# Decoding 64-bit weights by half words: raw loads two bytes off a word, one step of the decode on ScalarE

## The chip, the core and the metric

The kernel runs on one core of a Trainium2 chip. The metric is the device time of one execution in microseconds; the time before is the median of three runs.

## What is computed

An attention block masked by clusters feeds two expert layers without routing:

```
x = attention(q, k, v, centroids)                 # 1536 tokens x 512
h = x @ w_in;  g = h * sigmoid(1.702 h);  x = g @ w_out      # 512 -> 2048 -> 512
h = x @ w_in2; r = max(h, 0);             x = (r*r) @ w_out2
```

All inputs are float32 by value, but the four expert weights arrive as 64-bit floats. Before a weight can be multiplied it is turned into a 32-bit float on the chip with integer operations: keep the sign, clamp the magnitude to the range of a 32-bit float, rebias the exponent, shift the fraction.

## The kernel before

**Stages.** Attention takes the first 242 us or so. The expert layers follow as 32 slots: 2 layers x 2 batch halves x 8 pairs of hidden chunks (q = 0 to 31). A slot multiplies tokens with w_in for two hidden chunks (PSUM tiles `ph` and `ps`, L143 or L977), passes them through the activation (`active`, L840: ScalarE reads PSUM and writes `gh` and `h`), takes the rounding rest `gl` on VectorE (`low`, L851), and multiplies with w_out into `y` (L865 to L871). Every product is made of three float32r products of high and low parts. A slot has two halves of one `ph` bank each; a bank can be written again only once `active` has read it.

**Weights.** There are 64 weight chunks of 128 x 512 elements, 512 KB each. `w_dma` (L76) loads one from HBM into one of three buffers `raw64` from SyncE's queue. `magnitude` (L85) makes ScalarE write the absolute value of the high words into the target tile. `decode` (L90) does the four VectorE steps below, one at a time when the slot's hand-written order calls `step(k)` (L1018). The target is `wb` (a w_in chunk that stays), `rr`/`room` (the rest), or for four chunks in attention the raw buffer itself. Then a w_in chunk is stored to HBM by `keep` (L125) and split into `wxh` (ScalarE cast, L946) and `wxl` (VectorE, L947); a w_out chunk is split into `oh` and `ol` (`parts`, L108). `step` calls `fetch` (L996), the next raw load, when a decode is over.

```
nc.scalar.activation(f32(t), f32(raw)[:, :, 1], ACTF.Abs)            # L87  ScalarE
tensor_scalar(tf, tf, E_LO, E_HI, max, min)                          # L96  clamp
tensor_scalar(t, t, 3, 0x3FFFFFF8, shift_left, and)                  # L98  shift
scalar_tensor_tensor(t, high, 0xC0000000, t, and, or)                # L101 sign bits
scalar_tensor_tensor(t, low, 29, t, shift_right, or)                 # L104 fraction
```

**Order.** The order on each engine is written by hand (`manual_schedule`), instructions of an engine run in that order, and waits are semaphores between engines. Four chunks are decoded during attention and a fifth at its end (L797). `COUNTS` (L981) says how many are decoded in each later slot: 2 in slot 0, 4 in each of slots 1 to 6, 1 in slot 7, then 1 to 3 in slots 8 to 23 (3 in slots 9 and 18). Slots 0 to 7 are plain; from slot 8 on a slot uses sums of weights (`sums`, L937, VectorE into `wt`) to save products. In slots of layer 1 ScalarE first copies a product out of PSUM through a Relu (L845).

Of the kernel before, what the change touches and what calls it, by code (L numbers as in the profile page):

```python
# [11 lines left out]
F32 = mybir.dt.float32  # L12
BF16 = mybir.dt.bfloat16
U32 = mybir.dt.uint32
F32R = mybir.dt.float32r
ACTF = mybir.ActivationFunctionType
ALU = mybir.AluOpType
# [8 lines left out]

E_LO = float(np.uint32(0x38000000).view(np.float32))
E_HI = float(np.uint32(0x47EF0000).view(np.float32))


def f32(ap):
    return ap.bitcast(F32)
# [3 lines left out]
def tile_kernel(ctx, tc, q, k, v, cent, w_in1, w_out1, w_in2, w_out2, cw_cols, out):  # L36
    nc = tc.nc
    B, H, S, D = q.shape
    C = cent.shape[1]
    NT, DM = out.shape  # L40
    DFF = w_out1.shape[0]

    w_in1, w_out1, w_in2, w_out2 = (w.bitcast(U32) for w in (w_in1, w_out1, w_in2, w_out2))
    P = 128
    NJ = S // P
    G = 2
    KD = DM // P
# [7 lines left out]
    xpool = ctx.enter_context(tc.tile_pool(name="xpool", bufs=1))  # L55
    rpool = ctx.enter_context(tc.tile_pool(name="rpool", bufs=1))
    t3_p = ctx.enter_context(tc.tile_pool(name="t3", bufs=8))
    wraw_p = ctx.enter_context(tc.tile_pool(name="wraw", bufs=1))
    tmp_p = ctx.enter_context(tc.tile_pool(name="tmpw", bufs=1))
# [8 lines left out]


    x1 = [xpool.tile([P, KD, S], F32, name=f"x1_{b}") for b in range(B)]  # L70


    def raw_tile(at):
        return (wraw_p, wraw_p, tmp_p)[at].tile([P, DM, 2], U32, tag=f"raw{at}", name="raw64")

    def w_dma(w, fc, first, at):  # L76
        raw = raw_tile(at)
        if first:
            nc.sync.dma_start(raw.rearrange("p (a n) t -> p a (n t)", a=KD),
                              w[:, 2 * fc * P:2 * (fc + 1) * P].rearrange("(a p) f -> p a f", p=P))  # L80
        else:
            nc.sync.dma_start(raw.rearrange("p n t -> p (n t)"), w[fc * P:(fc + 1) * P, :])
        return raw

    def magnitude(raw, t):  # L85

        nc.scalar.activation(f32(t), f32(raw)[:, :, 1], ACTF.Abs)  # L87
        return raw, t

    def decode(raw, t, steps=range(4), inside=False):  # L90

        low, high, tf = raw[:, :, 0], raw[:, :, 1], f32(t)
        for i in steps:
            if i == 0:

                nc.vector.tensor_scalar(out=tf, in0=tf, scalar1=E_LO, scalar2=E_HI, op0=ALU.max, op1=ALU.min)  # L96
            elif i == 1:
                nc.vector.tensor_scalar(out=t, in0=t, scalar1=3, scalar2=0x3FFFFFF8,  # L98
                                        op0=ALU.logical_shift_left, op1=ALU.bitwise_and)
            elif i == 2:  # L100
                nc.vector.scalar_tensor_tensor(out=t, in0=high, scalar=0xC0000000, in1=t,  # L101
                                               op0=ALU.bitwise_and, op1=ALU.bitwise_or)
            else:
                nc.vector.scalar_tensor_tensor(out=low if inside else t, in0=low, scalar=29, in1=t,  # L104
                                               op0=ALU.logical_shift_right, op1=ALU.bitwise_or)
        return tf

    def parts(tf, hi, lo, engine=nc.gpsimd, held=None):  # L108

        nc.scalar.copy(hi, tf)  # L110
        rest = lambda: engine.tensor_tensor(out=lo, in0=tf, in1=f32(hi), op=ALU.subtract)
        if held is None:
            rest()
        else:
            held.append(rest)
# [692 lines left out]
    with ExitStack() as actx:  # L808
        w1, raw, xs, mags, first, last_norm = attention(actx)
# [180 lines left out]
    wo = {(0, 0): w1[2:]}  # L990
# [49 lines left out]
    keep(0, 2, f32(mags[4][1]))  # L1040
    weights[1].plain(0, f32(mags[4][1]).rearrange("p (a n) -> p a n", a=2))
    wo[0, 1] = out_tiles(1)
    parts(f32(mags[3][0])[:, :, 0], *wo[0, 1], nc.vector)
    fetch()
    fetch()

# [5 lines left out]
    for q, (layer, b, p) in enumerate(slots):  # L1052
# [3 lines left out]
        n = COUNTS[q] if q < len(COUNTS) else 0  # L1056
# [20 lines left out]
        if q + 2 < 2 * NP and q in PLAIN and q or q >= 2 * NP - 1 and more:  # L1077
            at = q + 1 + (q in PLAIN)
# [271 lines left out]
```

## Time and profile before

| what | value |
|---|---|
| time, median of 3 runs | 754.14 us (753.55 to 754.98) |
| the profiled execution's own time | 753.29 us |
| its span in the profile | 751.5 us |
| TensorE busy | 745.2 us, 99% |
| VectorE busy | 592.1 us, 79% |
| ScalarE busy | 504.0 us, 67% |
| GpSimd busy | 163.0 us, 22% |
| clock granted to TensorE | 1.00 in every stretch |

The span runs from the first to the last instruction; the 1.8 us between span and time lie around it. A busy share is an average over stages of different make-up, so the shares are read again by stretch below. In the trace lists, a row has the start, the duration, the engine, the line, the operation, what it writes and reads, and in brackets how long the engine stood idle before it and for whom it waited. A matmul's listed duration is longer than its step to the next one, because matmuls overlap.

### The profile page before, as it was taken

What the parts mean: (1) busy time and instruction counts of PE and PEld (TensorE: products, weight loads), DVE (VectorE), ACT (ScalarE), POOL (GpSimd) and SP (SyncE); (2) the same over time, 40 slices, a digit from 0 to 9 for tenths busy, and PEclk for the clock granted to TensorE, in tenths of its full rate; (3) what the DMA queues carried; (4) which work ended last, traced back from release to release, by engine and by line L of the source; (5) the groups of instructions that cost most, each with busy time, mean ns of one, the idle gap of its engine ahead of it and who ended that gap; (6) DMA issues with size and microseconds to landing.
All of it is one profiled execution on the core that took longest, in us unless ns stands there. A gap on an engine that the chain in (4) does not pass through costs nothing.

```text
span 751.5 us, 12136 instructions
## 1 busy us (share of the span) xinstructions
PE 745.2 (99%) x4345; PEld 684.6 (91%) x4345; DVE 592.1 (79%) x1079; ACT 504.0 (67%) x1049; POOL 163.0 (22%) x221
## 2 busy tenths in 40 slices
PE   8999999999999999999999999999999999999997
PEld 5999999999999999999999999998998989989996
DVE  7999999989897888887988877888878886643441
ACT  7999999999898644543765554676656675644441
POOL 5748667568654100000000000000000000000000
PEclk9999999999999999999999999999999999999999
DMA  9796796874320845555453432314442204011002
GB/s 206 189 205 145 141 202 179 175 188 109 83 59 12 231 141 173 160 158 172 151 155 124 139 123 91 113 43 136 159 140 85 84 29 140 29 31 54 1 1 84
DMA packets 72092, 90.90 MB, mean 121 GB/s; under 512 B 30368, under 2 KB 54080, under 8 KB 71936
## 3 DMA queue, kind: packets, MB, share of 16 engines
q1 hardware_dynamic: 71488, 89.99, 43.2%
q8 instruction: 34, 0.56, 0.3%
q14 instruction: 26, 0.21, 0.1%
q10 hardware_dynamic: 544, 0.13, 0.1%
HBM read 61.12 MB, written 13.94 MB: 100 GB/s over the span
## 4 chain that ended last, share of the span: by engine, by line
PE 97%; DVE 1%; ACT 1%; POOL 0%; issue 0%; POOLq 0%
PE ps L977 23%; PE y L871 18%; PE y L865 12%; PE pa L546 9%; PE pt L521 8%; PE y L867 6%; PE ps L497 5%; PE ph L143 4%; PE ps L499 4%; PE ps L143 4%; PE ps L350 1%; PE pt L287 1%; PE pm L376 1%; PE y L143 1%; PE ps L360 0%; DVE nm L503 0%
## 5 line engine op out<-in xcount | busy, mean ns | idle before, releaser
L534 DVE TENSOR_TENSOR el<-pt,eh 128x384 fp32r<-128x384 f32 x192 | 97.4, 549 | 7.2 <-ACT eh L531 6.4
L503 DVE TENSOR_REDUCE nm<-ps 128x1 f32<-128x768 f32 x96 | 91.4, 953 | 12.8 <-PE ps L499 10.8
L512 ACT ACTIVATE e<-ps,nm 128x768 f32<-128x768 f32 x96 | 87.8, 915 | 3.2 <-DVE nm L503 2.5
L531 ACT CAST eh<-pt 128x384 fp32r<-128x384 f32 x192 | 83.3, 490 | 7.3 <-PE pt L521 6.0
L848 ACT ACTIVATE gh<-h 128x384 fp32r<-128x384 f32 (+1 forms) x58 | 38.3, 660 | 68.6 <-DVE h L838 38.7
L852 DVE TENSOR_TENSOR gl<-h,gh 128x384 fp32r<-128x384 f32 (+1 forms) x104 | 67.0, 645 | 17.7 <-ACT h L849 9.9
L521 PE MATMUL pt<-identF,e 128*128 128x128 f32 x576 | 80.1, 274 | 0.1
L871 PE MATMUL y<-oh,gl 128*128 128x512 f32 x192 | 75.2, 392 | 0.0
L871 PE MATMUL y<-ol,gh 128*128 128x512 f32 x192 | 75.1, 391 | 0.0
L871 PE MATMUL y<-oh,gh 128*128 128x512 f32 x192 | 74.7, 389 | 0.0
L497 PE MATMUL ps<-k,q 128*128 128x512 f32 x192 | 68.9, 362 | 0.8 <-ACT e L512 0.8
L521 PEld LDWEIGHTS pt<-identF,e 128*128 128x128 f32 x576 | 65.3, 140 | 2.3 <-DVE el L534 1.4
L499 PE MATMUL ps<-k,q 80*128 80x512 f32 x192 | 60.8, 340 | 0.0
L947 DVE TENSOR_TENSOR wxl<-wb,wxh 128x512 fp32r<-128x512 f32 x37 | 25.5, 690 | 40.3 <-ACT wxh L946 31.7
L865 PE MATMUL y<-gh,ol 128*128 128x512 f32 x128 | 50.0, 391 | 0.0
L865 PE MATMUL y<-gh,oh 128*128 128x512 f32 x128 | 50.0, 391 | 0.0
L865 PE MATMUL y<-gl,oh 128*128 128x512 f32 x128 | 50.0, 391 | 0.0
L977 PE MATMUL ps<-xl,wxh 128*128 128x384 f32 x192 | 49.0, 336 | 0.0
L977 PE MATMUL ps<-xh,wxh 128*128 128x384 f32 x192 | 49.0, 336 | 0.0
L977 PE MATMUL ps<-xh,wxl 128*128 128x384 f32 x192 | 48.9, 335 | 0.0
L838 DVE CUSTOM_DVE_ANT_0 h<-ps,h 128x384 f32<-128x384 f32 x48 | 25.7, 552 | 29.0 <-PE ps L977 29.0
L546 PE MATMUL pa<-eh,v 128*128 128x384 f32 x192 | 47.3, 361 | 0.0
(233 smaller groups left out, 1921.2 us busy)
## 6 DMA issues: line engine op xcount, KB each, us to landing
raw<-in_moe_w_in_dram SPq DMA_DIRECT2D x32, 512.0 KB, 4.2
raw<-in_moe_w_out_dram SPq DMA_DIRECT2D x32, 512.0 KB, 3.7
wb<-wst SPq DMA_DIRECT2D x24, 512.0 KB, 3.3
q<-k SPq DMA_DIRECT2D x15, 384.0 KB, 5.6
wst<-room SPq DMA_DIRECT2D x16, 256.0 KB, 2.2
wst<-wb SPq DMA_DIRECT2D x13, 256.0 KB, 2.4
k<-k SPq DMA_DIRECT2D x16, 192.0 KB, 5.9
rawv<-in_v_dram SPq DMA_DIRECT2D x8, 384.0 KB, 7.3
```

Of the source, the lines that this page charges most:

```text
L143: nc.tensor.matmul(ph, w[a][:, kc * P:(kc + 1) * P], xs[kc][z][:, i * QB:(i + 1) * QB], start=(j == 0), stop=(j == len(terms) - 1))
L497: nc.tensor.matmul(ps[:, a:a + n], q2[:, qs], k2[:, a:a + n], start=True, stop=False)
L499: nc.tensor.matmul(ps[:, a:a + n], q1[0:K1, qs], k1[0:K1, a:a + n], start=False, stop=True)
L503: nc.vector.tensor_reduce(out=nm, in_=live["s", t][:, 0:S], op=ALU.max, axis=AX, negate=True)
L512: nc.scalar.activation(e, live["s", t][:, 0:S], ACTF.Exp, bias=live.pop(("nm", t)), accum_out=sums[:, s:s + 1])
L521: nc.tensor.transpose(pt[:, i], e[:, kc * P:(kc + 1) * P], identF)
L531: nc.scalar.copy(place("eh", t, u), live["pt", t, u])
L534: nc.vector.tensor_tensor(out=place("el", t, u), in0=live.pop(("pt", t, u)), in1=f32(place("eh", t, u)), op=ALU.subtract)
L546: nc.tensor.matmul(pa, v2[:, i % NJ, :], src[:, i % NJ, :], start=(i == 0), stop=(i == 2 * NJ - 1))
L865: nc.tensor.matmul(y[m], l[:, cs], r[:, 0:512], start=first, stop=last)
L871: nc.tensor.matmul(y[m], l[:, m * P:(m + 1) * P], r, start=(begin and z == 0), stop=(fc == KF - 1 and z == 2))
L977: nc.tensor.matmul(ps, w[a][:, wi, kc * P:(kc + 1) * P], x[z][kc], start=start and j == kc == 0, stop=j == 2 and kc == 1, skip_group_check ...
```

## The change

The raw buffer gets one more pair of words, and the load puts the 64-bit numbers two bytes behind a word boundary, as 16-bit elements. Each number is then cut differently: its top 16 bits lie at the start of a word of their own with the next number's first bits behind them, and the word before holds the 32 bits under them. ScalarE takes the absolute value of the top half words alone (as bf16) into a contiguous 16-bit tile `code`; VectorE clamps that tile of half words; ScalarE turns the half words into whole numbers with scale 2^19 and a bias from a new tile `base` (Identity, written as int32), which puts exponent and first fraction bits in place; VectorE then sets the rest of the fraction (shift right by 13, or) and, in a last operation on half words, the sign. One VectorE instruction of each of the 64 decodes goes, one ScalarE instruction comes. `base` is set once on GpSimd.

```diff
+STEP, BASE = float(2**19), float(0x3800 * 2**19)
...
-    w_in1, w_out1, w_in2, w_out2 = (w.bitcast(U32) for w in (w_in1, w_out1, w_in2, w_out2))
+    w_in1, w_out1, w_in2, w_out2 = (w.bitcast(U16) for w in (w_in1, w_out1, w_in2, w_out2))
...
+    base = xpool.tile([P, 1], F32, name="base")
+    nc.gpsimd.memset(base, -BASE)
...
-        return (wraw_p, wraw_p, tmp_p)[at].tile([P, DM, 2], U32, tag=f"raw{at}", name="raw64")
+        return (wraw_p, wraw_p, tmp_p)[at].tile([P, DM + 1, 2], U32, tag=f"raw{at}", name="raw64")
...
     def w_dma(w, fc, first, at):
         raw = raw_tile(at)
+        dst = raw.rearrange("p n t -> p (n t)").bitcast(U16)[:, 1:1 + 4 * DM]
...
-            nc.sync.dma_start(raw.rearrange("p n t -> p (n t)"), w[fc * P:(fc + 1) * P, :])
+            nc.sync.dma_start(dst, w[fc * P:(fc + 1) * P, :])
...
+    def words(raw):
+        top = raw.rearrange("p n t -> p (n t)").bitcast(U16).rearrange("p (n t) -> p n t", t=4)[:, 1:, 0]
+        return raw[:, 0:DM, 1], top
     def magnitude(raw, t):
-        nc.scalar.activation(f32(t), f32(raw)[:, :, 1], ACTF.Abs)
+        code = t.bitcast(U16)[:, DM:]
+        nc.scalar.activation(code.bitcast(BF16), words(raw)[1].bitcast(BF16), ACTF.Abs)
     def decode(raw, t, steps=range(4), inside=False):
...
             if i == 0:
-                nc.vector.tensor_scalar(out=tf, in0=tf, scalar1=E_LO, scalar2=E_HI, op0=ALU.max, op1=ALU.min)
+                size = code.bitcast(BF16)
+                nc.vector.tensor_scalar(out=size, in0=size, scalar1=E_LO, scalar2=E_HI, op0=ALU.max, op1=ALU.min)
             elif i == 1:
-                nc.vector.tensor_scalar(out=t, in0=t, scalar1=3, scalar2=0x3FFFFFF8,
-                                        op0=ALU.logical_shift_left, op1=ALU.bitwise_and)
+                nc.scalar.activation(t.bitcast(I32), code, ACTF.Identity, scale=STEP, bias=base)
             elif i == 2:
-                nc.vector.scalar_tensor_tensor(out=t, in0=high, scalar=0xC0000000, in1=t,
+                nc.vector.scalar_tensor_tensor(out=to, in0=rest, scalar=13, in1=t,
+                                               op0=ALU.logical_shift_right, op1=ALU.bitwise_or)
+            else:
+                half = high if inside else t.bitcast(U16)[:, 1::2]
+                nc.vector.scalar_tensor_tensor(out=half, in0=top, scalar=0x8000, in1=half,
                                                op0=ALU.bitwise_and, op1=ALU.bitwise_or)
```

The changed kernel's lines are numbered anew: L98 is the absolute value (before L87), L110 the clamp, L112 the new Identity, L114 the fraction, L118 the sign. Everything behind `decode` stands 14 lines further down: L862 and L863 are `active`, L866 `low`, L960 and L961 the split of w_in, L859 the Relu. TensorE's and SyncE's orders are as before.

Three places show what moves. First, ScalarE in a half of a plain slot, from one `wxh` cast to the next; before:

```order
L946 CAST wxh<-wb 128x512
L87 ACTIVATE wb<-raw_4252 128x512
L848 ACTIVATE gh<-ps 128x384
L849 ACTIVATE h<-ps 128x384
L87 ACTIVATE rr<-raw_4326 128x512
L848 ACTIVATE gh<-ps 128x384
L849 ACTIVATE h<-ps 128x384
L110 CAST oh<-rr 128x512
L946 CAST wxh<-wb 128x512
```

and with the change:

```order
L960 CAST wxh<-wb 128x512
L98 ACTIVATE wb<-raw_4254 128x512
L112 ACTIVATE wb<-wb,base 128x512
L862 ACTIVATE gh<-ps 128x384
L863 ACTIVATE h<-ps 128x384
L98 ACTIVATE rr<-raw_4328 128x512
L112 ACTIVATE rr<-rr,base 128x512
L862 ACTIVATE gh<-ps 128x384
L863 ACTIVATE h<-ps 128x384
L124 CAST oh<-rr 128x512
L960 CAST wxh<-wb 128x512
```

The Identity stands right behind the absolute value, ahead of the activation that frees the next `ph` bank, and between the two lies VectorE's clamp.

Second, VectorE in such a half, from `wxl` to the end of the second decode; before:

```order
L947 TENSOR_TENSOR wxl<-wb,wxh 128x512
L96 TENSOR_SCALAR wb<-wb 128x512
L98 TENSOR_SCALAR wb<-wb 128x512
L852 TENSOR_TENSOR gl<-h,gh 128x384
L101 SCALAR_TENSOR_TENSOR wb<-raw_4087,wb 128x512
L104 SCALAR_TENSOR_TENSOR wb<-raw_4087,wb 128x512
L96 TENSOR_SCALAR rr<-rr 128x512
L98 TENSOR_SCALAR rr<-rr 128x512
L852 TENSOR_TENSOR gl<-h,gh 128x384
L101 SCALAR_TENSOR_TENSOR rr<-raw_4161,rr 128x512
L104 SCALAR_TENSOR_TENSOR rr<-raw_4161,rr 128x512
```

and with the change:

```order
L961 TENSOR_TENSOR wxl<-wb,wxh 128x512
L110 TENSOR_SCALAR wb<-wb 128x512
L866 TENSOR_TENSOR gl<-h,gh 128x384
L114 SCALAR_TENSOR_TENSOR wb<-raw_4089,wb 128x512
L118 SCALAR_TENSOR_TENSOR wb<-raw_4089,wb 128x512
L110 TENSOR_SCALAR rr<-rr 128x512
L866 TENSOR_TENSOR gl<-h,gh 128x384
L114 SCALAR_TENSOR_TENSOR rr<-raw_4163,rr 128x512
L118 SCALAR_TENSOR_TENSOR rr<-raw_4163,rr 128x512
```

One instruction per decode is gone; the `gl` that remains between the clamp and the next step is that of the earlier bank.

Third, ScalarE in slot 18, around the third decode; before:

```order
L848 ACTIVATE gh<-h 128x768
L849 ACTIVATE h<-h 128x768
L87 ACTIVATE room<-raw_6707 128x512
L946 CAST wxh<-wt 128x512
L845 ACTIVATE h<-ps 128x384
```

and with the change:

```order
L862 ACTIVATE gh<-h 128x768
L863 ACTIVATE h<-h 128x768
L98 ACTIVATE room<-raw_6709 128x512
L112 ACTIVATE room<-room,base 128x512
L960 CAST wxh<-wt 128x512
L859 ACTIVATE h<-ps 128x384
```

The Identity now stands ahead of the `wxh` cast and of the Relu copy that frees a PSUM bank, and the clamp that it waits for stands on VectorE behind the four sums of `wt` and a `gl`.

## Rows read from the trace of the kernel before

**Rows 1.** The page's part 1: busy time, share of the span and instructions by engine.

```profile
PE 745.2 (99%) x4345; PEld 684.6 (91%) x4345; DVE 592.1 (79%) x1079; ACT 504.0 (67%) x1049; POOL 163.0 (22%) x221
```

**Rows 2.** The page's part 4: engine shares of the chain that ended last.

```profile
PE 97%; DVE 1%; ACT 1%; POOL 0%; issue 0%; POOLq 0%
```

**Rows 3.** TensorE's waits by line and releaser: us in total, times, longest.

```profile
PE pz L194 <- DVE zeros L188: 1.2, 1, 1.2
PE ps L497 <- ACT e L512: 0.8, 1, 0.8
```

**Rows 4.** Busy time by stretch: us, busy by engine, clock, DMA share, GB/s.

```profile
120.00:200.00 80.00, 80.00 (x558) 75.62 (x558) 71.56 (x122) 74.90 (x178) 54.13 (x71) 1.00 0.64 152
...
300.00:400.00 100.00, 100.00 (x577) 93.75 (x577) 84.52 (x158) 55.10 (x108) 0.00 (x0) 1.00 0.49 157
```

**Rows 5.** ScalarE's groups by line, shapes kept apart: xcount, busy us, mean ns.

```profile
L87 ACT ACTIVATE room<-raw 128x512 f32<-128x512 f32 x32 | 21.6, 675 | 0.0
...
L301 ACT ACTIVATE full<-pt,kq_scale 128x384 f32<-128x384 f32 x27 | 16.1, 598 | 0.0
...
L356 ACT COPY st<-ps 128x384 f32<-128x384 f32 x14 | 6.8, 486 | 0.3
```

**Rows 6.** VectorE's decode lines: ns min/median/max, first and last start.

```profile
L96 DVE TENSOR_SCALAR room<-room x32: 414/418/428, 368.0 to 602.5; 128x512 f32<-128x512 f32 x32
...
L98 DVE TENSOR_SCALAR room<-room x32: 426/428/430, 368.4 to 603.0; 128x512 uint32<-128x512 uint32 x32
...
L101 DVE SCALAR_TENSOR_TENSOR room<-raw,room x32: 681/685/693, 368.9 to 605.2; 128x512 uint32<-128x512 uint32 x32
...
L101 DVE SCALAR_TENSOR_TENSOR wb<-raw,wb x13: 681/686/2217, 249.1 to 346.3; 128x512 uint32<-128x512 uint32 x13
```

**Rows 7.** ScalarE at a plain half slot's start: start us, us, instruction, idle before.

```profile
310.48 0.62 ACT L946 CAST wxh<-wb 128x512 fp32r<-128x512 f32 x1 [2.21 <-PE ph L143]
```

**Rows 8.** All engines in the first slot, 240 to 259 us.

```profile
241.58 0.20 ACT L794 ACTIVATE warm<-identF 128x1 f32<-128x1 f32 x1
...
252.06 0.62 ACT L946 CAST wxh<-wb 128x512 fp32r<-128x512 f32 x1 [2.41 <-DVE wb L104]
...
256.32 0.51 ACT L849 ACTIVATE h<-ps 128x384 f32<-128x384 f32 x1
...
242.36 0.69 DVE L104 SCALAR_TENSOR_TENSOR raw<-raw,raw 128x512 uint32<-128x512 uint32 x1
...
243.08 0.41 SPq L79 DMA_DIRECT2D raw<-in_moe_w_in_dram  x1
...
244.36 0.85 PE L143 MATMUL y<-xh,wyh 128*128 128x384 f32 x4
...
258.92 0.85 PE L143 MATMUL ph<-xh,wxh 128*128 128x384 f32 x4
```

**Rows 9.** All engines in slot 7, 357 to 359 us.

```profile
358.25 0.48 ACT L849 ACTIVATE h<-ps 128x384 f32<-128x384 f32 x1
...
357.27 0.43 DVE L96 TENSOR_SCALAR rr<-rr 128x512 f32<-128x512 f32 x1 [0.73 <-ACT rr L87]
...
358.54 0.68 DVE L101 SCALAR_TENSOR_TENSOR rr<-raw,rr 128x512 uint32<-128x512 uint32 x1
...
358.82 0.93 PE L143 MATMUL ph<-xh,wxh 128*128 128x384 f32 x4
```

**Rows 10.** All engines in slot 18, 535 to 538 us.

```profile
537.02 0.49 ACT L845 ACTIVATE h<-ps 128x384 f32<-128x384 f32 x1 [0.98 <-PE ps L977]
...
535.91 0.95 DVE L852 TENSOR_TENSOR gl<-h,gh 128x768 fp32r<-128x768 f32 x1
...
537.86 0.51 PE L977 MATMUL ps<-xh,wxh 128*128 128x384 f32 x2
```

**Rows 11.** The page's part 6, weight loads: xcount, KB each, us to landing.

```profile
raw<-in_moe_w_in_dram SPq DMA_DIRECT2D x32, 512.0 KB, 4.2
raw<-in_moe_w_out_dram SPq DMA_DIRECT2D x32, 512.0 KB, 3.7
```

More of the change, by code (lines that the diff above doesn't have):

```diff
@@ L14 @@
 U32 = mybir.dt.uint32
+U16 = mybir.dt.uint16
+I32 = mybir.dt.int32
 F32R = mybir.dt.float32r
@@ L78, in w_dma @@
         if first:
-            nc.sync.dma_start(raw.rearrange("p (a n) t -> p a (n t)", a=KD),
-                              w[:, 2 * fc * P:2 * (fc + 1) * P].rearrange("(a p) f -> p a f", p=P))
+            nc.sync.dma_start(dst.rearrange("p (a n) -> p a n", a=KD),
+                              w[:, 4 * fc * P:4 * (fc + 1) * P].rearrange("(a p) f -> p a f", p=P))
         else:
-            nc.sync.dma_start(raw.rearrange("p n t -> p (n t)"), w[fc * P:(fc + 1) * P, :])
+            nc.sync.dma_start(dst, w[fc * P:(fc + 1) * P, :])
@@ L83, in w_dma @@
         return raw
+    def words(raw):
+        top = raw.rearrange("p n t -> p (n t)").bitcast(U16).rearrange("p (n t) -> p n t", t=4)[:, 1:, 0]
+        return raw[:, 0:DM, 1], top
     def magnitude(raw, t):
-        nc.scalar.activation(f32(t), f32(raw)[:, :, 1], ACTF.Abs)
+        code = t.bitcast(U16)[:, DM:]
+        nc.scalar.activation(code.bitcast(BF16), words(raw)[1].bitcast(BF16), ACTF.Abs)
         return raw, t
     def decode(raw, t, steps=range(4), inside=False):
-        low, high, tf = raw[:, :, 0], raw[:, :, 1], f32(t)
+        rest, top = words(raw)
+        to = rest if inside else t
+        high = raw.rearrange("p n t -> p (n t)").bitcast(U16).rearrange("p (n t) -> p n t", t=4)[:, 0:DM, 3]
+        code = t.bitcast(U16)[:, DM:]
@@ L100, in decode @@
             elif i == 2:
-                nc.vector.scalar_tensor_tensor(out=t, in0=high, scalar=0xC0000000, in1=t,
+                nc.vector.scalar_tensor_tensor(out=to, in0=rest, scalar=13, in1=t,
[3 more added lines that the diff above has]
+                nc.vector.scalar_tensor_tensor(out=half, in0=top, scalar=0x8000, in1=half,
                                                op0=ALU.bitwise_and, op1=ALU.bitwise_or)
-            else:
-                nc.vector.scalar_tensor_tensor(out=low if inside else t, in0=low, scalar=29, in1=t,
-                                               op0=ALU.logical_shift_right, op1=ALU.bitwise_or)
@@ L106, in decode @@
-        return tf
+        return f32(t)
     def parts(tf, hi, lo, engine=nc.gpsimd, held=None):
@@ L1042, in tile_kernel @@
     wo[0, 1] = out_tiles(1)
-    parts(f32(mags[3][0])[:, :, 0], *wo[0, 1], nc.vector)
+    parts(f32(words(mags[3][0])[0]), *wo[0, 1], nc.vector)
     fetch()
```

## The prediction

> **What bounds the kernel now.** I read the busy times first, then the chain that ended last, then TensorE's own waits, then the busy times by stretch. TensorE is busy 745.2 of 751.5 us, 99% [rows 1], and 97% of the chain that ended last lies on it [rows 2]. It waits only twice for long, 1.2 and 0.8 us, and neither time for a weight [rows 3]. Its clock is granted in full in attention (120 to 200 us) and in the plain slots (300 to 400 us), and in both it is busy without a gap [rows 4]. So the change can win nothing large: what it takes from VectorE is not on the path. What it can do is make TensorE wait, where a weight or a freed PSUM bank comes too late. There the chain ScalarE to VectorE to ScalarE counts, not the sum of either engine. That ScalarE waits 2.21 us for TensorE at the start of a plain half slot shows the room there [rows 7].
>
> **Busy time.** VectorE loses 64 shifts of 0.428 us [rows 6] and gets cheaper clamps; ScalarE gets 64 Identities.
>
> - *Identity.* No row shows it. A cast of 128x512 takes 0.62 us [rows 7]. A per-partition pointer costs 598 - 486 = 112 ns between two ScalarE forms of 128x384 from PSUM, one with and one without [rows 5]. Taken: 0.62 + 0.11 = 0.73 us. Bounds: 0.62 (the pointer is free) and 0.675 + 0.112 = 0.79 (it starts from the absolute value's 675 ns [rows 5]). ScalarE in all: 64 x 0.73 = +47 us, 504 to about 551.
> - *Clamp of half words.* 128x512 takes 0.418 us as float32 with one tensor operand, 0.685 with two [rows 6]. If the two-operand form moves one element and the one-operand form two in a step, 0.267 us are 256 steps and 0.151 us are fixed. My estimate is that half the bytes take half the steps again: 0.151 + 0.133 = 0.285 us. Bounds: 0.15 (only the fixed part) and 0.69 (one element in a step). The nearest row is the float clamp's 0.418, which I hold for the likelier miss.
> - *Sign on half words.* Two strided operands, taken as the 0.685 of the word form [rows 6]. Bounds: 0.42 (the one-operand rate) and 1.37 (twice).
> - VectorE in all: 64 x (0.428 + 0.418 - 0.285) = -36 us, 592 to about 556.
> - *Absolute value on 16-bit elements:* taken as 0.675; it reads the same bytes apart. *`base`:* one small fill on GpSimd at the start, before TensorE's first data are there: nothing, at most 0.1 us.
>
> **The chain of one decode.** Before, from the clamp's start to L101's start in slot 7, 358.54 - 357.27 = 1.27 us, with the shift and a `gl` between [rows 9]. Now: clamp 0.285, hand-over 0.04, Identity 0.73, hand-over 0.04, so 1.10 us, while the `gl` of the other bank fits beside the Identity. So where nothing else interferes the decode gets shorter by about 0.17 us, though it crosses engines twice more. In plain half slots (two decodes each) this hides entirely, and their 2.21 us of room grows. Cost: 0. The cover is TensorE's work of the half; with a clamp of 0.69 a half would be some 0.5 us longer than before, still inside the room.
>
> The cost lies elsewhere: the Identity stands on ScalarE ahead of casts and activations that TensorE waits for, and it waits for VectorE. Three places have too little room.
>
> **Slot 0 to 1** [rows 8]. The fifth decode's clamp is long done, but its Identity can start only when ScalarE is through its function table and the `warm` at 241.58 + 0.20, about 241.70, and ends at 242.43. The two VectorE steps then end at 242.47 + 0.73 + 0.68 = 243.88, against 242.36 + 0.69 = 243.05: +0.83. The cast `wyh` behind it ends at 243.92 + 0.62 = 244.54, so TensorE's `wyh` product moves from 244.36 to 244.60: **+0.24**. The next raw load, issued at 243.08, is late by the same 0.83, and nothing up to the `wxh` cast at 252.06 absorbs it, since each step there waited for the one before. The loads and GpSimd's part behind it move with it; the L101 that took 2.217 us beside GpSimd [rows 6] is slow again. From `wxh` at 252.89: its `wxl`, a clamp, an Identity and two VectorE steps for `wb` end at 256.81; only then comes the clamp of `rr` (to 257.00), and its Identity to 257.77 stands ahead of the x cast and of the activation whose last instruction, at 256.32 before, frees the bank. It now ends at 259.28 instead of 256.83. TensorE wants that bank at 258.92, 259.16 with the first delay, and starts at 259.33: **+0.17**.
>
> **Slot 7** [rows 9]. Two decodes into one buffer follow each other; the earlier one ends about 0.5 us sooner. The second's absolute value starts at 356.08, the clamp ends at 357.08 and the Identity at 357.85. Behind it come the x cast and two activation steps, 0.73 + 0.37 us from start to start, and the last, at 358.25 before, ends at 359.33. TensorE's second bank, which started at 358.82 just behind it, starts at 359.40: **+0.58**.
>
> **Slot 18** [rows 10]. The third decode's clamp stands behind the four sums and the `gl` of 535.91. All that moves up by about 0.35, to 535.55, because a shift is gone before it. The clamp runs from 536.43 to 536.72, the Identity from 536.76 to 537.49. The `wxh` cast starts at 537.39, and the Relu copy, at 537.02 before, starts at 537.91 and ends at 538.40. TensorE overwrites that bank at 537.86; it starts at 538.45: **+0.59**.
>
> **Elsewhere.** In attention ScalarE is busy 74.9 of 80 us and VectorE 71.6 [rows 4]; four Identities fall there, and I take 0 for them, with 0 to +0.1 us each as bounds. The other slots from 8 on have fewer decodes and gaps before the copies that TensorE waits for: 0, bounds -0.3 (small waits go) and +0.5.
>
> **Sum.** 0.24 + 0.17 + 0.58 + 0.59 = +1.58 us on the profiled execution's own 753.29, that is 754.87. The median of the runs is 754.14, 0.85 above that execution, so against it I forecast **755.7 us**. Bounds of the likeliest case: six Identities lie on these paths, so 0.62 gives -0.66 and 0.79 gives +0.36; five clamps, so 0.42 instead of 0.285 gives +0.66. With all of that +0.9 to +2.6: 755.0 to 756.7. A measurement of this kernel tells about 0.2%, 1.5 us, from no change; the forecast lies on that edge.
>
> **Rivals.**
>
> 1. *All of it hides: 754.1.* If the three places have more room than I read (the profile infers which semaphore came last, and TensorE shows no wait by name there [rows 3]), there is no change, give or take 0.5. Against it: TensorE's second bank in slot 7 starts 0.09 us after the activation ends [rows 9].
> 2. *Half words are dear: 757.5 to 760.* A clamp at 0.69 costs 0.40 more in five places, +2.0; a sign step at 1.37 costs 0.69 more in four, +2.8: 757.7 and 758.5. It decides once either goes over 0.6 or 0.9 us. For it: the fastest operation that the trace shows is 0.418 for this size [rows 6].
> 3. *The loads get slower: 759.9 at twice the time.* A w_in load lands after 4.2 us, a w_out load after 3.7 [rows 11]. The one issued at 243.08 is on the path of slot 1 [rows 8], so all that it gains in length TensorE waits for: +4.2 if it takes twice as long. From three times on the three raw buffers would not keep up in the plain slots, and the loss would be tens of us. No row here shows a load off a word. A milder form: a w_in load comes in pieces of 128 numbers of 8 bytes, 1 KB each, and if every piece off its place costs a quarter more, the load takes 5.2 us, TensorE waits 1.05 longer, and the time is 756.7. The Trainium skill, "DMA: Bandwidth & Descriptors", section "How a descriptor splits into AXI transactions", says that a transaction starts at a multiple of 256 bytes and that a piece which does not costs extra, which for 1 KB makes five transactions of four, the quarter of the milder form; it shows this for reads, and here the write side is off. No run so far shows it.
> 4. *Faster: 752.5.* VectorE's 36 us could shorten something that TensorE waits for. All its waits in the open are 2.0 us, for `zeros` and `e` [rows 3], and neither comes from a decode. It would have to be waits too short to be listed, adding up to 1.6 us.
>
> **Chances.** The forecast 0.50, of which 0.28 lies above the edge of 0.2% and 0.22 below; rival 1 0.23; rival 2 0.12; rival 3 0.10 (half milder, half twice); rival 4 0.05. Slower: 0.28 + 0.12 + 0.10 = 0.50. Same: 0.22 + 0.23 = 0.45. Faster: 0.05. The range 753.8 to 758.9 leaves out rival 4, the low end of rival 1 (0.04), loads of twice the time (0.05) and the dearest half words (0.03): 0.17.
>
> **What would show it.** In the changed profile: Identity near 0.73 us, clamp near 0.285, sign step near 0.69; ScalarE near 551 us, VectorE near 556; TensorE's steps at about 244.60, 259.33 and 359.8 (with the earlier delay in it), and a wait before the Relu's bank in slot 18; raw loads still at 4.2 and 3.7 us. The forecast is wrong if TensorE starts these without a gap, if a plain half slot waits, or if the loads take longer.

## The result: slower, and by three times the forecast

| | median | range of runs |
|---|---|---|
| before | 754.56 us | 753.55 to 755.28 |
| changed | 759.24 us | 757.57 to 760.13 |

The ratio is 1.006, with a 95% interval from 1.0037 to 1.0084: slower by 4.7 us where 1.58 were forecast. In the profiled executions the span grows from 751.5 to 755.9 us. The profile's busy times and the chain that ended last, of the changed kernel:

```profile
PE 748.2 (99%) x4345; PEld 685.7 (91%) x4345; DVE 562.7 (74%) x1015; ACT 546.8 (72%) x1113; POOL 163.5 (22%) x222
...
PE 90%; DVE 4%; ACT 2%; DMA 1%; issue 1%; SPq 1%; POOL 0%; DVEq 0%; POOLq 0%
```

They answer to [rows 1, 2]. VectorE lost 29 us and ScalarE gained 43, near the 36 and 47 of the forecast, and TensorE is still the engine that counts; but its share of the chain fell from 97% to 90%. TensorE's waits by line and releaser (us in total, times, longest) show places that [rows 3] did not have:

```profile
PE ph L157 <- ACT h L863: 0.8, 2, 0.5
...
PE ps L991 <- ACT h L859: 0.2, 1, 0.2
```

Both programs issue the same 4345 matmuls in the same order, so each can be paired with its twin and its start compared. That is the view which places the whole loss (my own arithmetic on the two traces' start times; gaps that differ by over 40 ns are called waits, smaller differences steps; a step is the time from one matmul's start to the next one's):

| from the twin's start before | later by | what happened since the last line |
|---|---|---|
| 139 us | -0.06 us | |
| 142 | 0.38 | one wait in attention |
| 256 | 0.53 | |
| 262 | 1.43 | two waits in slot 1 |
| 358 | 1.92 | no wait, matmul steps a few ns longer |
| 360 | 2.62 | one wait in slot 7 |
| 486 | 3.04 | longer steps |
| 498 | 3.52 | waits in slots 15 and 16 |
| 537 | 3.49 | |
| 540 | 3.95 | one wait in slot 18 |
| 747 | 4.27 | longer steps |

From 242 us on, the differences over 40 ns add up to 2.22 us and the small ones to 1.73. So the loss has two parts: waits, which the prediction looked for, and steps, of which it had no term at all. A second trace of the kernel before (b_again, below) shows how far such differences can be trusted: it is 1.4 us behind the first one by 256 us, through the start and attention, and then stays within 0.1 us of it to the end. So the expert layers can be read to a tenth of a microsecond, the sum over attention cannot.

**The decode's own steps** (minimum, median and maximum ns, then first and last start). From the views of the lines of the changed kernel:

```profile
L98 ACT ACTIVATE room<-raw x32: 636/674/695, 369.4 to 605.8; 128x512 bf16<-128x512 bf16 x32
...
L110 DVE TENSOR_SCALAR room<-room x32: 279/285/301, 370.6 to 606.6; 128x512 bf16<-128x512 bf16 x32
...
L112 ACT ACTIVATE room<-room,base x32: 706/716/726, 371.7 to 607.7; 128x512 int32<-128x512 uint16 x32
...
L114 DVE SCALAR_TENSOR_TENSOR room<-raw,room x32: 681/688/693, 372.4 to 609.9; 128x512 uint32<-128x512 uint32 x32
...
L118 DVE SCALAR_TENSOR_TENSOR room<-raw,room x32: 748/756/769, 373.1 to 610.6; 128x512 uint16<-128x512 uint16 x32
...
L118 DVE SCALAR_TENSOR_TENSOR raw<-raw x1: 1319/1319/1319, 137.9 to 137.9; 128x512 uint16<-128x512 uint16 x1
```

Against [rows 5, 6]: the clamp of half words takes 285 ns, as estimated, the Identity 716 for 730. The sign step on half words takes 756 instead of the 685 taken for it, and once, in place in a raw buffer, 1319.

**Attention.** That one, with what runs beside and behind it, in the trace of all engines:

```profile
137.88 1.32 DVE L118 SCALAR_TENSOR_TENSOR raw<-raw 128x512 uint16<-128x512 uint16 x1
...
138.04 1.32 POOL L405 TENSOR_TENSOR sim<-sim,mx 128x192 f32<-128x192 f32 x1 [1.47 <-DVE mx L404]
...
140.01 0.90 ACT L526 ACTIVATE e<-ps,nm 128x768 f32<-128x768 f32 x1 [0.66 <-DVE nm L517]
...
140.44 1.01 PE L535 MATMUL pt<-identF,e 128*128 128x128 f32 x6
```

It belongs to the one decode of attention that writes into the raw buffer from which it reads; it runs beside a GpSimd instruction that takes 1.32 us here. In the kernel before, a word operation stood there, and both were shorter:

```profile
137.87 0.68 DVE L104 SCALAR_TENSOR_TENSOR raw<-raw,raw 128x512 uint32<-128x512 uint32 x1
...
138.03 0.89 POOL L391 TENSOR_TENSOR sim<-sim,mx 128x192 f32<-128x192 f32 x1 [1.49 <-DVE mx L390]
```

The neighbour alone does not make it long. The sign steps of the three decodes before, which read one raw buffer and write another, stand beside the same GpSimd instruction, and take 0.74 or 0.75 us in every trace that has them, beside 0.91 or 0.92. One of them:

```profile
51.68 0.74 DVE L118 SCALAR_TENSOR_TENSOR raw<-raw,raw 128x512 uint16<-128x512 uint16 x1
...
51.84 0.92 POOL L405 TENSOR_TENSOR sim<-sim,mx 128x192 f32<-128x192 f32 x1 [1.49 <-DVE mx L404]
```

So it goes with the form, half words read and written in one buffer; whether that form is as long with GpSimd idle, no run shows. The row maximum behind it on VectorE comes late, the exponentials on ScalarE wait 0.66 us for it, and TensorE's transposes start at 140.44 instead of 140.24 and are then held once more. All the changed kernel's relatives below that keep this step have the delay between 139 and 142 us, 0.36 to 0.49 us and once 0.72, and no kernel with the old decode has it (0.00 in three).

**Slot 1**, in start order by engine:

```profile
244.26 0.41 SPq L85 DMA_DIRECT2D raw<-in_moe_w_in_dram  x1
...
243.84 0.62 ACT L124 CAST wyh<-raw 128x512 fp32r<-128x512 f32 x1
...
243.47 0.76 DVE L118 SCALAR_TENSOR_TENSOR raw<-raw,raw 128x512 uint16<-128x512 uint16 x1
...
249.10 0.67 ACT L98 ACTIVATE wb<-raw 128x512 bf16<-128x512 bf16 x1 [1.45 <-DMA raw<-in_moe_w_in_dram]
...
253.84 0.62 ACT L960 CAST wxh<-wb 128x512 fp32r<-128x512 f32 x1 [1.47 <-DVE wb L118]
...
255.54 0.72 ACT L112 ACTIVATE wb<-wb,base 128x512 int32<-128x512 uint16 x1 [0.50 <-DVE wb L110]
...
257.10 0.48 ACT L863 ACTIVATE h<-ps 128x384 f32<-128x384 f32 x1
...
259.71 0.48 ACT L863 ACTIVATE h<-ps 128x384 f32<-128x384 f32 x1
...
257.63 0.96 PE L157 MATMUL ph<-xh,wxh 128*128 128x384 f32 x4
...
260.24 0.96 PE L157 MATMUL ph<-xh,wxh 128*128 128x384 f32 x4 [0.26 <-ACT h L863]
```

The load is issued 1.18 us later than in [rows 8], 0.33 of it carried over from attention, 0.85 for the 0.83 worked out. But `wyh` comes when it did before (243.84 against 243.51, the same 0.33 later as everything) and starts while the fifth decode's last step, of 243.47, still runs: it reads an earlier chunk, and the first delay of the forecast does not exist. The load then takes 4.82 us from issue to landing where it took 4.36 (4.36 to 4.63 in four traces with the old decode), and the `wxh` cast is 1.78 us later than before. Its decode's Identity, at 255.54, stands ahead of the activation that ends at 257.58, and TensorE's first bank starts behind that, at 257.63; the second bank waits for 260.19 in the same way. Against the twins that is 0.36 us at the first bank and 0.53 at the second. The second is 0.3 to 0.6 us late in every kernel below that keeps the Identity in this place; the first goes with the load: it is on time in the second trace of the changed kernel, where the load takes 4.46 us.

**Slots 7 and 18:**

```profile
360.87 0.48 ACT L863 ACTIVATE h<-ps 128x384 f32<-128x384 f32 x1
...
361.41 0.96 PE L157 MATMUL ph<-xh,wxh 128*128 128x384 f32 x4 [0.49 <-ACT h L863]
```

```profile
541.16 0.47 ACT L859 ACTIVATE h<-ps 128x384 f32<-128x384 f32 x1
...
541.68 0.61 PE L991 MATMUL ps<-xh,wxh 128*128 128x384 f32 x2 [0.16 <-ACT h L859]
```

The two places answer to [rows 9, 10]: the activation ends and TensorE starts 0.05 us later, as the prediction read it; the delays against the twin are 0.66 and 0.43 us for 0.58 and 0.59 forecast.

### The profile page after: what moved, and what is told of

It is laid out like the page before. It is cut to its first block, busy times and chain, and to the rows that moved or that the text cites. A ratio compares the mean times of both kernels' runs of the same rounds, so it can differ in the third digit from the quotient of the medians.

```text
span 755.9 us, 12160 instructions
## 1 busy us (share of the span) xinstructions
PE 748.2 (99%) x4345; PEld 685.7 (91%) x4345; DVE 562.7 (74%) x1015; ACT 546.8 (72%) x1113; POOL 163.5 (22%) x222
## 4 chain that ended last, share of the span: by engine, by line
PE 90%; DVE 4%; ACT 2%; DMA 1%; issue 1%; SPq 1%; POOL 0%; DVEq 0%; POOLq 0%
PE ps L991 23%; PE y L885 17%; PE y L879 11%; PE pa L560 8%; PE pt L535 8%; PE y L881 5%; PE ps L511 4%; PE ps L513 4%; PE ph L157 4%; PE ps L157 3%; PE ps L364 1%; PE pt L301 1%; DVE nm L517 1%; DMA raw<-in_moe_w_in_dram 1%; PE pm L390 1%
## 5 line engine op out<-in xcount | busy, mean ns | idle before, releaser
L866 DVE TENSOR_TENSOR gl<-h,gh 128x384 fp32r<-128x384 f32 (+1 forms) x104 | 66.9, 644 | 17.7 <-ACT h L863 9.9
L862 ACT ACTIVATE gh<-h 128x384 fp32r<-128x384 f32 (+1 forms) x58 | 38.2, 659 | 47.8 <-DVE h L852 26.6
L961 DVE TENSOR_TENSOR wxl<-wb,wxh 128x512 fp32r<-128x512 f32 x37 | 25.6, 691 | 35.9 <-ACT wxh L960 32.4
L879 PE MATMUL y<-gl,oh 128*128 128x512 f32 x128 | 50.3, 393 | 0.0
L879 PE MATMUL y<-gh,ol 128*128 128x512 f32 x128 | 50.2, 392 | 0.0
L879 PE MATMUL y<-gh,oh 128*128 128x512 f32 x128 | 50.2, 392 | 0.0
```

What stands on the lines that cost most here:

```text
L866: nc.vector.tensor_sub(g[1][:, at], h[:, c, at], f32(g[0][:, at]))
L879: nc.tensor.matmul(y[m], l[:, cs], r[:, 0:512], start=first, stop=last)
```

## The experiments

Three theories at the start: **A**, matmul steps became longer because tiles lie elsewhere; **B**, the hand-over to ScalarE and its place in the order make TensorE wait; **C**, loads off a word are slower. Four kernels on one chip first. Each set below ran with the kernel before beside it on its own chip (754.56 us in the first set, 754.46 in the second), and every ratio is to that.

**The changed kernel again.** The label of each kernel stands in brackets, since the expectations use them (this one is a_again).

> The changed kernel once more, beside the others of this set. Every theory: 757.5 to 760, with TensorE late by about 0.9 us more around 257 to 260 us, 0.66 at slot 7, 0.43 at slot 18. Open is how much of the 4.7 us the trace holds as waits (2.9 of 4.4 us in the first one) and how much as matmul steps that are each a little longer.

759.22 us (758.89 to 759.56), ratio 1.0058 [1.0045, 1.007]. The same waits appear, but for the one at slot 1's first bank, and the longer steps add up to 3.0 us in the expert layers instead of 1.6 (both against the second trace of the kernel before): the size of that part differs between executions of the same program.

**Layout alone (e1).** The kernel before with the longer buffers and the extra tile, loads and decode untouched:

```diff
+    base = xpool.tile([P, 1], F32, name="base")
+    nc.gpsimd.memset(base, 1.0)
...
-        ....tile([P, DM, 2], U32, ...)
+        ....tile([P, DM + 1, 2], U32, ...)
...
```

> The kernel before with nothing but its raw buffers one pair of words longer and the small tile and fill for the bias added: every later tile lies elsewhere in SBUF, no instruction changes. Theory A (part of the loss, 1.5 us, comes from matmul steps that got longer because their operands lie elsewhere): 756.0. Theory B (all of it is waits for the decode) and theory C (loads off a word): 754.6, within 0.5.

755.79 us, ratio 1.002 [1.0011, 1.0029], 1.2 us for a program with not one decode instruction changed. In its trace no wait appears behind 20 us but one of 0.05, and the steps grow as in the changed kernel. So the layout alone costs time, which theories B and C cannot explain; which operands count is taken up below.

**Loads on a word (e2).**

```diff
-        dst = ...bitcast(U16)[:, 1:1 + 4 * DM]
+        dst = ...bitcast(U16)[:, 0:4 * DM]
...
-        return raw[:, 0:DM, 1], top
+        return raw[:, 0:DM, 0], top
...
```

The decode's instructions keep their shapes, but they take the low word of each number whole, so this kernel leaves out fraction bits of the weights.

> The changed kernel with loads put back on a word boundary; the decode's instructions keep their shapes but take the low word of each number for the fraction, so the values lose fraction bits. Theory C (loads two bytes off a word are slower, above all the one that slot 1 waits for): 757.5 or less, raw loads shorter by some tenths of a us, TensorE 0.5 us less late at slot 1. Theories A and B: 759, as the changed kernel.

758.55 us (757.26 to 760.06), not told apart from 759.22. The load of slot 1 takes 4.68 us here, TensorE's banks there are late as before. Theory C falls. The page's loads of the changed kernel say the same, with 4.3 and 3.5 us against 4.2 and 3.7 in [rows 11]; the second trace of the kernel before has 4.3 and 3.5 as well:

```profile
raw<-in_moe_w_in_dram SPq DMA_DIRECT2D x32, 512.0 KB, 4.3
raw<-in_moe_w_out_dram SPq DMA_DIRECT2D x32, 512.0 KB, 3.5
```

**Rebias on VectorE (e3).**

```diff
-        code = t.bitcast(U16)[:, DM:]
+        code = t.bitcast(U16)[:, 1::2]
...
-                nc.scalar.activation(t.bitcast(I32), code, ACTF.Identity, scale=STEP, bias=base)
+                nc.vector.tensor_scalar(out=t.bitcast(I32), in0=code, scalar1=STEP, scalar2=-BASE, op0=ALU.mult, op1=ALU.add)
```

> The changed kernel with the rebias back on VectorE (multiply and add on the half words, which now lie in every second half word of the tile): no step of the decode crosses to ScalarE after the absolute value. Theory B (the hand-over to ScalarE and its place in ScalarE's order make TensorE wait): the waits at slots 1, 7 and 18 go, 756 to 757. Theory A: no more than that, since the 1.5 us of longer steps stay. Theory C: 758 or more.

757.13 us, ratio 1.0032 [1.002, 1.0045]: 2.1 less than the changed kernel. The waits at slots 1, 15, 16 and 18 are gone, one of 0.34 us at slot 7's first bank takes the place of the 0.66. Its steps:

```profile
L110 DVE TENSOR_SCALAR room<-room x32: 452/461/471, 371.0 to 606.1; 128x512 bf16<-128x512 bf16 x32
...
L112 DVE TENSOR_SCALAR room<-room x32: 426/427/430, 371.4 to 606.6; 128x512 int32<-128x512 uint16 x32
```

The rebias costs VectorE 427 ns against ScalarE's 716, and the clamp of half words that lie two apart 461 instead of 285. Theory B holds: without the crossing TensorE is free of those waits.

Then the two causes were mended apart and together.

**Order (e4).** Three Identities (and the VectorE steps behind them) set behind the activation:

```diff
+                    if u == 1 and q in (1, 7):
+                        do(0, (1, 2, 3))
...
-                    do(u, (0, 1))
+                    late_one = u == 0 and q in (1, 7)
+                    do(u, (0,) if late_one else (0, 1))
...
+            moved = n > 2 and long
...
-                do(2, (0, 1))
+                do(2, (0,) if moved else (0, 1))
...
+                if moved:
+                    do(2, (1, 2, 3))
...
```

> The changed kernel with three of its 64 Identities set later in ScalarE's order, behind the activation that frees the PSUM bank: the one for rr in slot 1, the one of slot 7, the third of slot 18; the VectorE steps behind them move with them. Theory B (an Identity standing ahead of that activation holds TensorE up): 0.42 + 0.65 + 0.43 = 1.5 us less than the changed kernel, 757.7. Theory A (those matmuls only start late because matmul steps before them are longer): 759.2.

757.32 us, ratio 1.0039 [1.0027, 1.0051]: 1.9 less than 759.22. Three delays (slot 1's second bank, slot 7, slot 18) are gone from the trace; the third came back in slot 19, where TensorE waits 0.4 us for a copy behind the next Identity, which had moved back with it, and is 0.67 us late against its twin.

**Padding (e5).**

```diff
-    base = xpool.tile([P, 1], F32, name="base")
+    base = xpool.tile([P, 16], F32, name="base")[:, 0:1]
-        ....tile([P, DM + 1, 2], U32, ...)
+        ....tile([P, DM + 8, 2], U32, ...)
...
```

In the built programs a tile takes a multiple of 32 bytes in each partition. So a `base` of one word moves everything behind it by 32 bytes, and a raw buffer that is 8 bytes longer moves what follows it by 32 more; the two numbers here make it 64 each.

> The changed kernel with the bias tile padded to 64 bytes and the raw buffers lengthened by 64 bytes instead of 8, so that all tiles behind them start at a multiple of 64 bytes again, as before the change; the instructions are the same. Theory A (matmuls whose x tiles start 32 bytes off such a multiple step 3 ns longer): 1.3 to 1.5 us less than the changed kernel, 757.8, with the steps at L157 3.4 ns shorter. Theory B (waits alone): 759.2.

756.68 us, ratio 1.003 [1.0019, 1.0041]: 2.5 less, for two numbers in tile shapes. TensorE's product into `ps` of a plain slot, by its starts, in the changed kernel and then in the padded one:

```profile
300.06 0.87 PE L157 MATMUL ps<-xh,wxh 128*128 128x384 f32 x4
300.76 0.87 PE L157 MATMUL ps<-xl,wxh 128*128 128x384 f32 x4
301.47 0.87 PE L157 MATMUL ps<-xh,wxl 128*128 128x384 f32 x4
```

```profile
301.77 0.86 PE L157 MATMUL ps<-xh,wxh 128*128 128x384 f32 x4
302.46 0.86 PE L157 MATMUL ps<-xl,wxh 128*128 128x384 f32 x4
303.16 0.86 PE L157 MATMUL ps<-xh,wxl 128*128 128x384 f32 x4
```

Four matmuls take 0.705 us in the one and 0.695 in the other. One by one: 173 to 174 ns each in the padded kernel, and 174 and 180 in turn in the changed one.

**Both (e6), and the padding with the rebias on VectorE (e7).** No edit but those of e4, e5 and e3.

> Both together, the padded tiles and the three Identities set later. If the two causes are separate and add: 759.2 - 1.4 - 1.5 = 756.3; the rest to 754.6 would then be slot 1's late load, attention (0.36) and slots 15 and 16 (0.3).

755.06 us, ratio 1.0011 [1.0003, 1.002]. From 759.22, that is 4.2 less, close to the 1.9 and 2.5 apart: two separate causes that add.

> The changed kernel with padded tiles and the rebias on VectorE, with the half words in every second half word of the tile. If causes are separate: 757.1 - 1.3 = 755.8. If it comes to 754.6 or less, half words on VectorE alone are no worse than the decode before; a faster time than before by over 0.2% is expected by no theory.

755.17 us (754.24 to 759.29), ratio 1.0014 [1.0003, 1.0025], for 757.13 without the padding.

**A second trace of the kernel before (b_again), its padded form (e8), and the large waits mended (e9).** e8 is e1 with the tile shapes of e5. e9 is e5 with the order of slots 1 and 7 changed as in e4, and this:

```diff
+                    if q == 1 and not u:
+                        for k in (1, 2, 3):
+                            step(k)
+                        absolute()
+                        step(4)
...
+            if n > 2 and long:
+                do(2, (0, 1))
             if long:
                 low(gb, 1, ALL)
...
-            elif i == 2:
+            elif i == (3 if inside else 2):
...
```

> The kernel before once more, for a second trace of it on this chip. Every theory: the same time as before within its spread, 753.5 to 756. Open is the start: in traces of the changed kernel the first matmuls, from 4.2 us on, step at half rate for up to 1.1 us, in the one trace of the kernel before they do not. If that is chance, it can show here too; if it belongs to the change, it does not.

754.67 us. The half-rate start shows in it too. The start of TensorE in the first trace before and in this one:

```profile
4.16 0.52 PE L287 MATMUL pt<-identF,rawkq 128*128 128x128 f32 x3
```

```profile
4.15 0.85 PE L287 MATMUL pt<-identF,rawkq 128*128 128x128 f32 x3
```

So it is chance and no part of the change. The first trace before was a good one, by 0.5 us at the start and by 0.8 more in attention, where TensorE starts 0.4 us late twice in the second.

> The kernel before with the longer raw buffers and the extra tile, but with the tile padded to 64 bytes and the buffers longer by 64 bytes, so that every tile starts at a multiple of 64 bytes, only further on. Theory A (the 32 bytes off such a multiple are what costs, not the place as such): 754.0 to 754.5, no slower than before; from the matmul steps of the padded changed kernel 0.4 us faster. If the place as such counts: 755.8, as with the unpadded layout.

753.48 us, ratio 0.9992 [0.9984, 1.0001]: not told apart from before, and not slower, while the unpadded layout cost 1.2.

> The changed kernel with padded tiles and every wait that the traces show mended by order: both Identities of slot 1 and that of slot 7 behind the activation, the third decode of slot 18 ahead of gl, and for the one decode in attention that runs beside GpSimd the fraction step last instead of the sign step. Theory B: 755.06 less 0.36 in attention, 0.45 at slot 1 and 0.4 at slots 18 and 19, 753.9, not slower than before. If the waits only move elsewhere: 755.

753.77 us, ratio 0.9993 [0.9984, 1.0002], 5.4 less than the changed kernel. Its waits and its chain:

```profile
PE pz L208 <- DVE zeros L202: 1.2, 1, 1.2
PE ps L511 <- ACT e L526: 0.8, 1, 0.8
```

```profile
PE 746.6 (99%) x4345; PEld 685.2 (91%) x4345; DVE 561.6 (75%) x1015; ACT 545.5 (72%) x1113; POOL 162.9 (22%) x222
...
PE 98%; DVE 1%; POOL 0%; ACT 0%; issue 0%; POOLq 0%
```

These are [rows 2, 3] again. By the twins, 0.25 us are left of the delay in attention and 0.4 in slots 15 and 16, against 0.5 us that the padded steps win. With its large waits mended the half-word decode is level with the one before, in its padded form (753.48) too, and 30 us less VectorE work make it no better: the time it saves was covered.

**Which tiles (e10 to e16).** My reading of theory A was that x tiles, which start 32 bytes off a multiple of 64 in the changed kernel, make their matmuls longer.

```diff
 (e5, but)
-        ....tile([P, DM + 8, 2], U32, ...)
+        ....tile([P, DM + 1, 2], U32, ...)
```

> The changed kernel with the bias tile padded to 64 bytes and the raw buffers only 8 bytes longer: the x tiles and rooms start at multiples of 64 bytes, and all tiles behind the raw buffers (q, k, e parts, oh, ol, gh, gl, the weight tiles) 32 bytes off one. If only the x tiles count: as the padded kernel, 756.7. If any operand that TensorE streams counts, 3 ns a matmul: the steps at L157 become normal and those of the y products and of attention grow, some 1,000 to 1,900 matmuls, so 759.5 to 762.

759.0 us, and the steps into `ps` at L157 are as long as in the changed kernel (176.6 ns on average), with the x tiles at multiples of 64. That reading falls. Four kernels with other sizes of the bias tile moved the later tiles (`base` of 40, 24, 72 and 104 words in place of one, raw buffers of DM + 1):

> The changed kernel with a bias tile of 160 bytes: the tiles behind the raw buffers stand 256 bytes further on than before the change, as in e5, but the x tiles 160 bytes further on, 32 off a multiple of 64. Theory D (the place of the later tiles counts): steps of the first layer's ps products at L157 as before, 0 +- 1 ns. Theory A (the x tiles' place counts): 3.4 ns longer each.

> The same with a bias tile of 96 bytes, the later tiles 192 bytes further on. Theory D by 256 bytes (0 and 256 short, 128 and 160 long): between, or long; if short, the long places are a narrow band around 128 and 160.

> The same with a bias tile of 288 bytes, the later tiles 384 bytes further on. Theory D by 256 bytes: long, 3.4 ns. If only 128 and 160 are bad and the place repeats by 512 or not at all: short.

> The same with a bias tile of 416 bytes, the later tiles 512 bytes further on. Theory D by 256 bytes or by 512: short, as before the change.

All four have the long steps into `ps` (176.6 to 176.7 ns) and take 757.5 to 759.3 us in one run each, so the later tiles' place does not decide either. What is common to every kernel with long steps is raw buffers of DM + 1, at least one of which stands 32 bytes off a multiple of 64.

So e10 with a gap of 8 words in front of the third raw buffer:

```diff
+    gap = tmp_p.tile([P, 8], F32, tag="gap", name="gap")
+    nc.gpsimd.memset(gap, 0.0)
```

> The changed kernel with the bias tile padded to 64 bytes, raw buffers 8 bytes longer and a gap of 32 bytes among them, so that the second and third raw buffer start 32 bytes off a multiple of 64 and every tile that TensorE reads at one. Theory E (any tile that TensorE reads, 32 off, sets the longer steps): short steps at L157, 173.3 ns, and 756.7 as the padded kernel. Theory F (the raw buffers' own places, through the loads into them): long steps, 176.7 ns every second one 6 ns longer, and 759.

758.95 us (758.17 to 760.94), steps of 175.5 to 176 ns, although every tile that TensorE reads in the plain slots stands at a multiple of 64. The reverse, e5 with `base` of one word and the gap in front of the first raw buffer:

> The changed kernel with raw buffers 64 bytes longer, all three at multiples of 64, and the bias tile not padded, so that the x tiles and rooms start 32 bytes off; a gap of 32 bytes sets the rest right. Theory F (the raw buffers' places decide): steps at L157 of 173.3 ns and 756.7, as the padded kernel. If the x tiles count too: 176.7 ns, 758 or more.

757.17 us (756.65 to 758.5), steps of 173.3 to 173.5 ns at that product. The same rows of both:

```profile
301.26 0.86 PE L159 MATMUL ps<-xh,wxh 128*128 128x384 f32 x4
301.96 0.87 PE L159 MATMUL ps<-xl,wxh 128*128 128x384 f32 x4
302.66 0.87 PE L159 MATMUL ps<-xh,wxl 128*128 128x384 f32 x4
```

```profile
301.77 0.86 PE L159 MATMUL ps<-xh,wxh 128*128 128x384 f32 x4
302.46 0.85 PE L159 MATMUL ps<-xl,wxh 128*128 128x384 f32 x4
303.15 0.85 PE L159 MATMUL ps<-xh,wxl 128*128 128x384 f32 x4
```

0.70 to 0.705 us a group in the first, 0.69 in the second. So in these products it is the raw buffers that decide, though TensorE never reads them. Whether it is their start or their length is not separated: all twelve traces with long steps are of buffers of DM + 1, all eight with short ones of DM or DM + 8, and no kernel has buffers of DM + 1 that all start at multiples of 64.

Of the same slots' products into `ph`, which read the same x tiles, the pattern is another. They step at 173.4 ns in the first trace of the changed kernel and at 176.7 in the second, where the products `y` at L879 are 0.9 us longer in all, for 0.2 in the first; the difference between 1.6 and 3.0 us lies there. The `ph` starts of the first trace and of the second:

```profile
308.46 0.86 PE L157 MATMUL ph<-xh,wxh 128*128 128x384 f32 x4
309.16 0.85 PE L157 MATMUL ph<-xl,wxh 128*128 128x384 f32 x4
```

```profile
309.64 0.87 PE L157 MATMUL ph<-xh,wxh 128*128 128x384 f32 x4
310.35 0.87 PE L157 MATMUL ph<-xl,wxh 128*128 128x384 f32 x4
```

The last kernel (e16) keeps some longer steps, 0.8 us in the expert layers against the second trace before, where the padded kernel is 0.5 us shorter and the changed one 1.6 longer. They lie in the `y` products of the plain slots, which read no x tile, and the second trace of the changed kernel has the like; that x tiles count is not shown. **Open** is how a buffer's place or length reaches the steps of matmuls that read other tiles: some longer steps (0.15 us) also occur behind 600 us, when no raw load is under way. No run here separates a cause.

## Why the prediction was wrong

- **What bounds the kernel** was right: TensorE. That nothing large could be won holds; with the large waits mended the time is that of before.
- **Busy times** were right: Identity 716 ns for 730, clamp 285 for 285. The sign step was mis-sized, 756 ns for 685 (bounds 420 and 1370); it adds 4.5 us to VectorE's sum.
- **Slot 7 and slot 18** were right in place and size: 0.66 and 0.43 us for 0.58 and 0.59. Setting the Identities behind the activation removed both, though slot 18's came back in slot 19.
- **Slot 0 to 1** was right in its mechanism, wrong in its terms. The +0.24 at `wyh` does not exist: I took its source for the fifth decode, and it reads an earlier chunk. The +0.17 came out as two delays, 0.36 at the first bank and 0.53 at the second: the load took 4.82 us instead of 4.36 and the sign step 0.07 longer, so that the first decode's Identity too stood ahead of an activation that TensorE was waiting for. The first of the two is in part chance, since with a load of 4.46 us it is gone.
- **"Elsewhere: 0"** failed twice. In attention one sign step, in place in a raw buffer and beside GpSimd, took 1.32 us and TensorE was 0.44 late; with the fraction step in its place (the kernel with the waits mended) that step takes 0.67 there, the GpSimd instruction 0.90, and 0.25 of the delay stay. I had priced only the Identities there and not asked what the new last step does in place. In slots 15 and 16 the decode before ends later and `oh`, `wxl` and `h` behind it follow: 0.4 us, inside the +0.5 of the bound but not in the sum.
- **The step that failed most** is the line that costs nothing because it is not there: the buffers' new length and the new tile were priced by their work ("`base`: one small fill") and not by where they put the others. It is worth 1.2 us alone (the layout alone) and 2.5 us in the changed kernel (the padding): more than the forecast itself. How the layout lengthens the matmul steps stays open.
- **Rivals.** Rival 1 is out, since all three places have the waits named. Rival 2 is out in size: neither operation passed its point (0.6 and 0.9 us), but for that one sign step. Rival 3 is out: loads off a word take as long as on one. By the rule that the Trainium skill, "DMA: Bandwidth & Descriptors", "How a descriptor splits into AXI transactions", gives for reads, the milder form would have held if it went for writes too; the trace does not show it for a write side two bytes off, at 4.3 and 3.5 us against 4.2 and 3.7. Rival 4 is out: 30 us off VectorE shorten nothing.

## What to carry to other kernels

Where one engine is busy 99%, look at every edit for what it puts ahead of the instruction that frees that engine's next bank, and set the new step behind it; and read the order of the queue it joins, since a step that costs its engine nothing can cost the bound engine its whole length. A buffer that grows by a few bytes moves tiles: pad it, so that all starts keep their alignment, before judging the idea (2.5 of 4.7 us here). When a loss is spread thin, pair the instructions of the two traces and split the difference into few large gaps and many small ones: they have different causes.

## What the runs showed of the hardware that I had not expected

- Matmuls of 384 columns step at 173 to 174 ns, or at 174 and 180 in turn, and this went with buffers that they do not read: the products into `ps` of the plain slots are short (173.3 ns on average) in the eight traces of kernels whose raw buffers all start at multiples of 64 bytes, long (175.7 to 176.7) in all twelve of kernels with buffers of DM + 1, at least one of them 32 bytes off.
- Two executions of one program differed by 1.4 us in such steps: the products into `ph` took 173.4 ns a step in one and 176.7 in the other, at a granted clock of 1.00 in that stretch of both.
- A sign step on half words that reads and writes one buffer takes 1.31 to 1.33 us beside a GpSimd instruction, which grows from 0.92 to 1.32; from one buffer to another it takes 0.74 beside the same instruction.
- ScalarE turns 16-bit whole numbers into 32-bit ones with scale and pointer bias at 716 to 725 ns for 128x512; VectorE does the same multiply and add in 427 (from half words two apart).
- VectorE's clamp of 128x512 bf16 takes 285 ns for half words in a row and 461 for half words two apart; a two-operand step on 16-bit elements four and two apart is slower (756 ns) than on words (688).
- A load of 512 KB that lands two bytes off a word takes no longer than one on it: 4.3 and 3.5 us, as in the second trace of the kernel before.
- In most traces, of the kernel before too, TensorE's first matmuls of 128 columns behind 4.2 us step at half rate (213 ns for 109) until 5 to 6.5 us, though the granted clock reads 1.00 there: 0.3 to 1.2 us of spread between executions.
